# Attention and MoE in one kernel: a new issue order for a turn of the attention loop, and other engines for five of its copies out of PSUM

## The chip, the cores and the metric

The kernel runs on one core of one Trainium2 chip. The metric is the device time of one execution in microseconds (us): before the change the median of three runs is 442.36 us (441.19 to 442.59). The engines are named as in the profile: TensorE is PE (its weight loads PEld), VectorE is DVE, ScalarE is ACT, GpSimd is POOL, and SyncE, which issues most DMAs, is SP.

## The reference

Block-causal attention over 8 batches of 8 heads (576 positions, 64 per head, in float32), then a mixture of experts over the 4608 resulting tokens: a gate picks one of 8 experts per token, each expert keeps its 80 highest gates, and the kept tokens go through two matrix products.

```python
scores = scale * np.matmul(q, k.transpose(0, 1, 3, 2))           # q, k, v: (8, 8, 576, 64)
scores = np.where(block_i >= block_j, scores, -1000000000.0)      # blocks of 64 positions
attn = np.exp(scores - np.max(scores, axis=-1, keepdims=True))
attn = attn / (np.sum(attn, axis=-1, keepdims=True) + 1e-09)
x = np.matmul(attn, v)  # then (4608, 512): tokens by heads * 64
...
logits = x @ w_gate                                              # (4608, 8)
expert_idx, gate_w = argmax and its softmax probability
for e in range(8):
    tok_idx = the 80 tokens of expert e with the highest gate_w
    out[tok_idx] = gate_w[tok_idx, None] * (np.maximum(x[tok_idx] @ w1[e], 0) @ w2[e])
```

## The kernel before

The attention works on 32 pairs of heads (4 pairs per batch). A pair is spread over several turns of one loop: turn `i` loads pair `i+3`, turns the q and k of pair `i+1` (`prep`, DVE transposes at L409, q scaled on POOL at L412), makes the scores and the softmax of pair `i`, and finishes pair `i-1`. Four pairs of heads make a batch, and so four turns.

The rows of a pair's 576 positions are cut into tiles 0 to 3 of 128 rows and tile 4 of 64 rows. In a turn PE runs, in this order: the scores of tile 3 (`scores "3"`, L427), `back C` of the pair before (L492), the scores of tiles 2 and 0 (`"20"`), `back 44` (L475), `values 0` (L522), the scores of tile 1, `back A`, `values 1`, the scores of tile 4 (`scores_4`, L443), `back B`. A `back` turns exponentials by a product with the identity into PSUM; a `take` (L532 on ACT, L534 on DVE) copies it to SBUF, where `values` needs it: `back C` to the tile PF, `A` and `B` to PT, `44` to pl. `values` multiplies by v, and its own `take` copies the result to xT.

`max` (L448, and L452 for tile 4) finds the row maxima of the scores on DVE, `soft` (L456, L461) takes the exponentials on ACT, and reads the row sum with a second small instruction. `flip` (L275) transposes xT on DVE for storing.

The scores have two buffers in PSUM, used in rotation: the scores of tile 1 go where those of tile 3 were, so they wait for both `soft` of tile 3; those of tile 4 wait for the `soft` of tiles 2 and 0. `back C` needs tile 4's `soft` of the turn before, and `values 0` needs both halves of `back C` taken. All other products of PE in a turn rotate over four PSUM buffers (`pm`).

Every four turns a finished batch leaves nine small jobs in a list, and each `step` of the loop runs the next: `recip`, `store`, `logits` (two products, L292), `logits2` (five transposes, L304, and DVE work at L310 and L319), `gate` (nine DVE instructions, L327 to L341, with one exponential on ACT between, L330), `turn` (POOL) and `turn2` (L358, L362). So in turns 6, 10, ... come the first logits, in the next turn the rest of the logits, in the one after (8, 12, ..., 28; "the gate turn" below) the gate, and the fourth has no job. After turn 31 there is one more gate turn, 32, without new scores, and then the last batch is finished by itself.

Nothing is scheduled by a planner here: within the loop (`tc.manual_schedule()`, L564) every engine's queue holds its instructions in the order in which the table TURN calls them, and TAKE says which engine copies: `"a"` is ACT, `"v"` is DVE. What follows the loop (choice of the kept tokens, gather, experts) hangs on its end.

Of the kernel before, what the change touches and what calls it, by code (L numbers as in the profile page):

```python
# [24 lines left out]
CHUNK = 80  # L25


TAKE = {"back": {"A0": "a", "A1": "v", "B0": "a", "B1": "v", "C0": "a", "C1": "a", "44": "a"},
        "values": {0: "a", 1: "a"}}

GROUPS = {"3": ((3, 0),), "20": ((2, 0), (0, 384)), "1": ((1, 0),)}

TURN = (
    (3, "load"),
    (0, "begin"),
    (1, "prep", 0),
    (0, "scores", "3"),
    (-1, "back", "C"),
    (0, "scores", "20"),
    (-1, "take", "back", "C0"),  # L40
    (-1, "take", "back", "C1"),
    (2, "load_v"),
    (0, "max", "3"),
    (0, "soft", 3, 1),
    (0, "soft", 3, 0),
    (0, "max", "20"),
    (0, "step"),
    (-1, "back", "44"),
    (-1, "values", 0),
    (0, "soft", 0, 0),  # L50
    (0, "scores", "1"),
    (0, "soft", 2, 1),
    (0, "back", "A"),
    (1, "prep", 1),
    (-1, "take", "back", "44"),
    (0, "soft", 2, 0),
    (0, "max", "1"),
    (0, "take", "back", "A1"),
    (0, "soft", 0, 1),
    (-1, "take", "values", 0),  # L60
    (0, "soft", 1, 0),
    (0, "soft", 1, 1),
    (-1, "values", 1),
    (0, "scores_4"),
    (0, "back", "B"),
    (-1, "take", "values", 1),
    (-2, "flip"),
    (0, "max_4"),
    (0, "take", "back", "B1"),
    (0, "take", "back", "A0"),  # L70
    (0, "step"),
    (0, "soft_4"),
    (0, "take", "back", "B0"),
    (0, "step"),
)

# [2 lines left out]
def tile_attn_moe(ctx, tc, q, k, v, w_gate, w1, w2, capacity, out, xs=None, dbg=None):  # L79
# [295 lines left out]
    class Pair:  # L375
# [153 lines left out]
        def take(self, what, x):  # L529

            if TAKE[what][x] == "a":
                nc.scalar.copy(*self.out.pop((what, x)))  # L532
# [576 lines left out]
```

## Time and profile before

| | us |
|---|---|
| median of three runs | 442.36 |
| the profiled execution, device time | 441.93 |
| its span, first to last instruction | 440.2 |
| PE busy | 409.2 (93%) |
| ACT busy | 288.3 (65%) |
| DVE busy | 280.1 (64%) |
| POOL busy | 65.9 (15%) |

The loop fills the span from 8 to about 316 us. Shares of the whole span mix it with the experts, where DVE and ACT have little to do; inside the loop both are busy about 17 of every 20 us. The chain of waits that the page prints ends in the output's DMA and tells nothing of the loop, so the loop is read from the timeline, one engine at a time, where each row has its start, its length and, in brackets, the idle time before it with what ended it.

### The profile page before, as it was taken

To read this page: it belongs to the slowest core of one execution; us is meant where nothing else is said; L and a number is where in the kernel's file an instruction comes from. 1 tells how busy PE (TensorE), PEld (TensorE's weight loads), DVE (VectorE), ACT (ScalarE), POOL (GpSimd) and SP (SyncE) were. 2 spreads that over 40 slices of the span, in tenths; PEclk is the share of its full clock that TensorE was granted. 3 is DMA by queue.
4 is the path that set the end of the run, shared out by engine and by line. 5 is a ranking of instruction groups with operands and counts; after the bars stand their busy time and mean duration, and the time that the engine had idled before them with its cause. 6 is when DMAs were issued, how large, how long until landed. Compare 5 with 4: busy or idle time off the path is not lost. (4 is left out here: it accounts for less than half of the span.)

```text
span 440.2 us, 14257 instructions
## 1 busy us (share of the span) xinstructions
PE 409.2 (93%) x5755; PEld 263.4 (60%) x5755; DVE 280.1 (64%) x559; ACT 288.3 (65%) x887; POOL 65.9 (15%) x133
## 2 busy tenths in 40 slices
PE   5899999999999999999999999999868899999970
PEld 3466666666666566666666656666546855666510
DVE  5677788888798888879879887986682131100000
ACT  1698888798788879888887887888520123333230
POOL 5001111011111101112111010210026201100000
PEclk9899999999999999999999999999997899999996
DMA  9677878988786998898879887854087999999000
GB/s 130 117 133 165 174 125 212 241 171 165 190 164 130 158 291 171 167 210 178 170 136 281 167 173 192 179 128 110 2 224 245 324 405 410 412 401 357 20 15 21
DMA packets 230168, 84.34 MB, mean 192 GB/s; under 512 B 196877, under 2 KB 215309, under 8 KB 230096
## 3 DMA queue, kind: packets, MB, share of 16 engines
q1 hardware_dynamic: 222528, 64.91, 63.5%
q0 software_dynamic: 5200, 18.16, 11.9%
q8 instruction: 47, 0.77, 0.7%
q10 hardware_dynamic: 2368, 0.30, 0.6%
q14 instruction: 25, 0.20, 0.1%
HBM read 63.21 MB, written 20.33 MB: 190 GB/s over the span
## 5 line engine op out<-in xcount | busy, mean ns | idle before, releaser
L456 ACT ACTIVATE P<-sc,negm 128x128 f32<-128x128 f32 (+3 forms) x256 | 133.4, 531 | 16.2 <-DVE negm L448 14.5
L448 DVE TENSOR_REDUCE negm<-sc 128x2 f32<-128x1024 f32 (+3 forms) x128 | 100.6, 811 | 38.5 <-PE sc L434 38.4
L427 PE MATMUL sc<-T,T 64*128 64x128 f32 (+3 forms) x512 | 94.6, 468 | 2.2 <-POOL T L412 1.3
L492 PEld LDWEIGHTS pm<-ident,P 64*128 64x128 f32 x1536 | 56.4, 139 | 33.1 <-ACT xT L532 11.0
L492 PE MATMUL pm<-ident,P 64*128 64x64 f32 x1536 | 68.8, 229 | 1.9 <-DVE prod L310 0.4
L522 PE MATMUL pm<-PT,vn 128*64 128x128 f32 (+1 forms) x512 | 60.7, 379 | 0.0
L427 PEld LDWEIGHTS sc<-T,T 64*128 64x128 f32 x512 | 42.6, 191 | 23.7 <-issue 7.2
L412 POOL TENSOR_SCALAR T<-T 128x576 f32<-128x576 f32 x32 | 21.4, 668 | 227.0 <-DVE T L409 227.0
L456 ACT ACTIVATION_READ_ACCUMULATOR P<-sc,negm 128x1 f32 x256 | 52.6, 205 | 0.0
L409 DVE STREAM_TRANSPOSE T<-ld 128x576 f32<-128x576 f32 x64 | 48.7, 763 | 1.4 <-DMA ld<-in_q_dram 1.4
L522 PE MATMUL pm<-PF,vn 128*64 128x64 f32 (+1 forms) x768 | 48.2, 247 | 0.9 <-ACT PF L532 0.9
L522 PEld LDWEIGHTS pm<-PT,vn 128*64 128x64 f32 x512 | 33.5, 137 | 22.9 <-issue 22.9
L884 PE MATMUL av<-w,hT 128*32 128x512 f32 (+1 forms) x320 | 43.1, 594 | 1.6 <-DVE y L889 1.6
L532 ACT COPY PF<-pm 128x512 f32<-128x512 f32 x64 | 34.4, 588 | 15.0 <-PE pm L492 15.0
L843 PE MATMUL ps<-xsT,w 128*64 128x80 f32 x1024 | 40.7, 239 | 3.7 <-issue 3.7
L534 DVE COPY PT<-pm 128x512 f32<-128x512 f32 x64 | 43.5, 680 | 0.3 <-PE pm L492 0.3
L843 PEld LDWEIGHTS ps<-xsT,w 128*64 128x64 f32 x1024 | 38.3, 141 | 7.5 <-issue 7.0
L889 DVE SCALAR_TENSOR_TENSOR y<-av,comb,yt 80x512 f32<-80x512 f32 x8 | 6.0, 746 | 57.2 <-ACT yt L887 51.0
L443 PE MATMUL sc<-T,T 64*64 64x288 f32 x256 | 39.0, 424 | 1.2 <-ACT P L456 1.2
L461 ACT ACTIVATE P<-sc,negm 128x576 f32<-128x576 f32 x32 | 23.7, 741 | 22.1 <-DVE negm L452 22.1
L532 ACT COPY PT<-pm 128x512 f32<-128x512 f32 x64 | 37.8, 591 | 0.0
L522 PEld LDWEIGHTS pm<-PF,vn 128*64 128x64 f32 x768 | 32.0, 137 | 7.4 <-ACT PF L532 1.1
(168 smaller groups left out, 419.2 us busy)
## 6 DMA issues: line engine op xcount, KB each, us to landing
w<-in_moe_w_dram SPq DMA_DIRECT2D x13, 2048.0 KB, 19.2
ld<-in_q_dram SPq DMA_DIRECT2D x128, 72.0 KB, 3.2
out_dram<-zero POOLq DMA_DIRECT2D x18, 512.0 KB, 3.8
xs<-Y SPq DMA_DIRECT2D x32, 288.0 KB, 4.9
ld<-in_k_dram SPq DMA_DIRECT2D x124, 72.0 KB, 2.8
vn<-in_v_dram SPq DMA_DIRECT2D x64, 128.0 KB, 3.0
w<-in_moe_w_dram POOLq DMA_DIRECT2D x3, 2048.0 KB, 11.1
vt<-in_v_dram SPq DMA_DIRECT2D x32, 32.0 KB, 2.9
```

The lines of the kernel that those rows point to most:

```text
L409: nc.vector.transpose(t, self.nat[x].rearrange("p g d -> p (g d)"))
L427: nc.tensor.matmul(s[:, h, c:c + P * (u + 1)], lhsT=self.T[0][r, P * u:P * (u + 1)], rhs=self.T[1][r, 0:P * (u + 1)], start=(x == 0), stop ...
L443: nc.tensor.matmul(s[r, c, 0:288], lhsT=self.T[0][r, 512:S], rhs=self.T[1][r, 288 * c:288 * (c + 1)], start=True, stop=True)
L448: nc.vector.tensor_reduce(self.negm[:, u], self.s[g][:, :, c:c + P * (u + 1)], axis=AX.X, op=ALU.max, negate=True)
L456: nc.scalar.activation(Pt[self.i % 2][u][:, h], self.s[g][:, h, c:c + P * (u + 1)], AF.Exp, bias=self.negm[:, u, h:h + 1], scale=1.0, accu ...
L461: nc.scalar.activation(Pt[self.i % 2][4][:, 0:S].rearrange("p (c k) -> p c k", c=2), self.s["4"][:, :, 0:288], AF.Exp, bias=self.negm[:, 4 ...
L492: nc.tensor.transpose(pt[c][:, n_ * BLK:(n_ + 1) * BLK], from_[r, P * j:P * (j + 1)], ident[r, r])
L522: nc.tensor.matmul(to, lhsT=lhs, rhs=rhs, start=(n_ == 0), stop=(n_ == len(steps) - 1))
L532: nc.scalar.copy(*self.out.pop((what, x)))
L534: nc.vector.tensor_copy(*self.out.pop((what, x)))
L843: yield nc.tensor.matmul(dst(b)[64 * c:64 * (c + 1)], lhsT=w_[:, a, col:col + 64], rhs=x_[:, a], start=(a == 0), stop=(a == n - 1))
L884: last = nc.tensor.matmul(to[col:col + s1 - s0], lhsT=hT[:, a, s0:s1], rhs=w_[:, a], start=(a == ends[0]), stop=(a == ends[1]), tile_posit ...
```

## The change

The order of the calls in a turn is another, and five copies change their engine: `A1` and `B1` go from DVE to ACT; `B0`, `values 0` and `values 1` go from ACT to DVE.

```diff
-TAKE = {"back": {"A0": "a", "A1": "v", "B0": "a", "B1": "v", "C0": "a", "C1": "a", "44": "a"},
-        "values": {0: "a", 1: "a"}}
+TAKE = {"back": {"A0": "a", "A1": "a", "B0": "v", "B1": "a", "C0": "a", "C1": "a", "44": "a"},
+        "values": {0: "v", 1: "v"}}
...
     (0, "begin"),
-    (1, "prep", 0),
+    (0, "step"),
     (0, "scores", "3"),
...
+    (0, "soft_4"),
+    (0, "back", "B"),
+    (0, "take", "back", "B0"),
     (0, "take", "back", "B1"),
-    (0, "take", "back", "A0"),
-    (0, "step"),
-    (0, "soft_4"),
-    (0, "take", "back", "B0"),
     (0, "step"),
 )
```

A turn still has three `step`s. Before they stood in the middle (after the maxima of tiles 2 and 0), between `max_4` and `soft_4`, and at the end; now they stand at the start, in the middle (before `back 44`, with the maxima of tiles 2 and 0 behind it), and at the end. Both `prep`s now come after the maxima of tiles 2 and 0, and the `take` of `44` comes before the `soft` of tile 3. Beside the jobs' own products, the order of PE in a turn is unchanged.

On DVE, in a gate turn and the end of the turn ahead of it (`mx` to `Gm` is the gate; `negm x3` are the maxima of tiles 3, 2 and 0; `T` is a `prep`), before:

```order
L452 TENSOR_REDUCE negm<-sc 128x1
L534 COPY PT<-pm 128x2x2x128
L310 TENSOR_TENSOR prod<-pm,rs 128x256
L310 TENSOR_TENSOR prod<-pm,rs 64x64
L319 TENSOR_REDUCE lg<-prod 128x40
L409 STREAM_TRANSPOSE T_2087<-ld_1740 128x576
L448 TENSOR_REDUCE negm<-sc 128x2 x3
L327 TENSOR_REDUCE mx<-lg 128x5
L329 TENSOR_TENSOR dl<-lg,mx 128x5x8
```

And now, in the same place:

```order
L452 TENSOR_REDUCE negm<-sc 128x1
L534 COPY PT<-pm 128x2x2x128
L310 TENSOR_TENSOR prod<-pm,rs 64x64
L319 TENSOR_REDUCE lg<-prod 128x40
L327 TENSOR_REDUCE mx<-lg 128x5
L329 TENSOR_TENSOR dl<-lg,mx 128x5x8
...
L341 TENSOR_TENSOR Gm<-eq,g 128x40
L448 TENSOR_REDUCE negm<-sc 128x2 x3
L409 STREAM_TRANSPOSE T_2158<-ld_1740 128x576
L409 STREAM_TRANSPOSE T_2202<-ld_1741 128x576
L448 TENSOR_REDUCE negm<-sc 128x2
```

The whole gate moved from behind the maxima of tiles 3, 2 and 0 to ahead of them, one `prep` moved behind them, and the larger of the two L310 moved into the turn before.

On ACT, around the gate's exponential (`dl`; PF is `take` of `back C`, `P ... 128x512` the exponentials of tile 3), before:

```order
L461 ACTIVATE P_1_130,sums_1427<-sc,negm 128x576
L532 COPY PT<-pm 128x2x2x128
L532 COPY PF<-pm 128x512 x2
L456 ACTIVATE P_0_128,sums<-sc,negm 128x512 x2
L330 ACTIVATE dl<-dl 128x5x8
L456 ACTIVATE P_0_123,sums<-sc,negm 128x128
```

And now:

```order
L461 ACTIVATE P_1_130,sums_1427<-sc,negm 128x576
L532 COPY PT<-pm 128x2x2x128
L330 ACTIVATE dl<-dl 128x5x8
L532 COPY PF<-pm 128x512 x2
L532 COPY pl_132<-pm 64x128
L456 ACTIVATE P_0_128,sums<-sc,negm 128x512 x2
```

The gate's exponential moved ahead of the two copies of `back C`, and the copy of `44` ahead of the exponentials of tile 3.

## Rows read from the trace of the kernel before

**Rows 1.** The head of the page: the span, and PE's busy time, share of the span and instructions.

```profile
span 440.2 us, 14257 instructions
...
PE 409.2 (93%) x5755; PEld 263.4 (60%) x5755; DVE 280.1 (64%) x559; ACT 288.3 (65%) x887; POOL 65.9 (15%) x133
```

**Rows 2.** The timeline of PE, from a turn without jobs (it starts at 130.50) and the two starts that follow it, to a gate turn (159.14 to 168.38). Columns: start in us, us, engine, line, operation, out<-in, shape, count.

```profile
130.50 1.13 PE L427 MATMUL sc<-T,T 64*128 64x512 f32 x4
...
131.50 0.71 PE L492 MATMUL pm<-ident,P 64*128 64x64 f32 x16
...
139.27 1.08 PE L427 MATMUL sc<-T,T 64*128 64x512 f32 x4
...
140.52 0.71 PE L492 MATMUL pm<-ident,P 64*128 64x64 f32 x16
...
158.45 0.77 PE L304 MATMUL pm<-ident,lgT 128*128 128x128 f32 x5
159.14 1.13 PE L427 MATMUL sc<-T,T 64*128 64x512 f32 x4
...
160.13 0.70 PE L492 MATMUL pm<-ident,P 64*128 64x64 f32 x16
...
161.98 0.44 PE L522 MATMUL pm<-PF,vn 128*64 128x128 f32 x4
...
164.30 0.70 PE L427 MATMUL sc<-T,T 64*128 64x256 f32 x4
...
166.21 1.19 PE L443 MATMUL sc<-T,T 64*64 64x288 f32 x8
167.33 0.84 PE L492 MATMUL pm<-ident,P 64*128 64x64 f32 x16
...
168.38 0.70 PE L427 MATMUL sc<-T,T 64*128 64x512 f32 x2
```

**Rows 3.** The timeline of DVE over the same gate turn, from tile 4's maximum of the turn before (157.92) to tile 1's maximum (165.89); idle time before a row in brackets.

```profile
157.92 0.76 DVE L452 TENSOR_REDUCE negm<-sc 128x1 f32<-128x576 f32 x1 [0.41 <-PE sc L443]
158.60 0.68 DVE L534 COPY PT<-pm 128x512 f32<-128x512 f32 x1
159.19 0.54 DVE L310 TENSOR_TENSOR prod<-pm,rs 128x256 f32<-128x256 f32 x2
159.77 0.74 DVE L319 TENSOR_REDUCE lg<-prod 128x40 f32<-128x320 f32 x1
160.42 0.77 DVE L409 STREAM_TRANSPOSE T<-ld 128x576 f32<-128x576 f32 x1
161.11 2.38 DVE L448 TENSOR_REDUCE negm<-sc 128x2 f32<-128x1024 f32 x3
163.42 0.18 DVE L327 TENSOR_REDUCE mx<-lg 128x5 f32<-128x40 f32 x1
163.63 0.20 DVE L329 TENSOR_TENSOR dl<-lg,mx 128x40 f32<-128x40 f32 x1
...
165.19 0.78 DVE L409 STREAM_TRANSPOSE T<-ld 128x576 f32<-128x576 f32 x1
165.89 0.65 DVE L448 TENSOR_REDUCE negm<-sc 128x2 f32<-128x512 f32 x1
```

**Rows 4.** The timeline of ACT in the same gate turn: the copies of `back C`, the exponentials of tile 3 with the reading of their sums, the gate's exponential.

```profile
160.86 1.07 ACT L532 COPY PF<-pm 128x512 f32<-128x512 f32 x2 [0.83 <-PE pm L492]
162.42 0.69 ACT L456 ACTIVATE P<-sc,negm 128x512 f32<-128x512 f32 x1 [0.49 <-DVE negm L448]
...
163.10 0.68 ACT L456 ACTIVATE P<-sc,negm 128x512 f32<-128x512 f32 x1
163.67 0.20 ACT L456 ACTIVATION_READ_ACCUMULATOR P<-sc,negm 128x1 f32 x1
163.87 0.24 ACT L330 ACTIVATE dl<-dl 128x40 f32<-128x40 f32 x1
164.01 0.35 ACT L456 ACTIVATE P<-sc,negm 128x128 f32<-128x128 f32 x1
```

**Rows 5.** Groups of instructions over the whole span, shapes kept apart (busy us, mean ns of one): the maximum of tile 3, and the only copy on DVE out of PSUM that is about as small as that of `values 1`.

```profile
L448 DVE TENSOR_REDUCE negm<-sc 128x2 f32<-128x1024 f32 x32 | 38.3, 1195 | 3.9 <-PE sc L434 3.9
...
L362 DVE COPY Wt<-pm 128x40 f32<-128x40 f32 x8 | 1.7, 215 | 2.3 <-PE pm L358 2.3
```

**Rows 6.** The timeline of all engines at the last gate turn, 32, after the scores have ended: DVE's tile 4 maximum, a `flip`, the gate's first instruction, and the first of `values 0` with what it waited for.

```profile
309.45 0.76 DVE L452 TENSOR_REDUCE negm<-sc 128x1 f32<-128x576 f32 x1 [1.10 <-PE sc L443]
...
311.96 0.76 DVE L275 STREAM_TRANSPOSE Y<-xT 128x576 f32<-128x576 f32 x1
312.65 0.15 DVE L327 TENSOR_REDUCE mx<-lg 128x5 f32<-128x40 f32 x1
...
313.02 0.44 PE L522 MATMUL pm<-PF,vn 128*64 128x128 f32 x4 [0.88 <-ACT PF L532]
```

**Rows 7.** The timeline of the first turn on ACT and PE: the reading of tile 3's second sum, the scores of tile 1 behind it, the exponentials of tile 0 and the scores of tile 4.

```profile
12.97 0.20 ACT L456 ACTIVATION_READ_ACCUMULATOR P<-sc,negm 128x1 f32 x1
...
13.22 0.70 PE L427 MATMUL sc<-T,T 64*128 64x256 f32 x4 [0.97 <-ACT P L456]
...
13.68 0.37 ACT L456 ACTIVATE P<-sc,negm 128x128 f32<-128x128 f32 x1 [0.51 <-DVE negm L448]
...
15.67 0.75 PE L443 MATMUL sc<-T,T 64*64 64x288 f32 x2 [1.19 <-ACT P L456]
```

More of the change, by code (lines that the diff above doesn't have):

```diff
@@ L35 @@
     (0, "begin"),
-    (1, "prep", 0),
+    (0, "step"),
     (0, "scores", "3"),
     (-1, "back", "C"),
+    (-1, "take", "back", "C1"),
     (0, "scores", "20"),
+    (0, "max", "3"),
     (-1, "take", "back", "C0"),
[L41 to L46, printed above, removed]
     (0, "step"),
@@ L49 @@
     (-1, "values", 0),
+    (0, "max", "20"),
+    (-1, "take", "back", "44"),
+    (0, "soft", 3, 0),
+    (0, "soft", 3, 1),
+    (0, "soft", 2, 0),
+    (1, "prep", 0),
     (0, "soft", 0, 0),
+    (0, "soft", 0, 1),
+    (2, "load_v"),
     (0, "scores", "1"),
+    (0, "back", "A"),
+    (-1, "values", 1),
     (0, "soft", 2, 1),
-    (0, "back", "A"),
     (1, "prep", 1),
-    (-1, "take", "back", "44"),
-    (0, "soft", 2, 0),
     (0, "max", "1"),
-    (0, "take", "back", "A1"),
-    (0, "soft", 0, 1),
-    (-1, "take", "values", 0),
     (0, "soft", 1, 0),
     (0, "soft", 1, 1),
-    (-1, "values", 1),
+    (-1, "take", "values", 0),
     (0, "scores_4"),
-    (0, "back", "B"),
+    (0, "take", "back", "A0"),
+    (0, "take", "back", "A1"),
     (-1, "take", "values", 1),
```

## The prediction

> **What bounds the kernel now.** I read the head of the page first: PE is busy 93% of the span [rows 1], so what other engines do counts only where PE waits for it. The busy share doesn't show where that is, so I read PE's timeline by starts, turn against turn. A turn without jobs takes 139.27 - 130.50 = 8.77 us, the gate turn 168.38 - 159.14 = 9.24 [rows 2]. Inside them nearly every product starts as long after the one before as in all other turns; PE streams. Two waits are left. First, behind a turn without jobs `back C` starts 140.52 - 139.27 = 1.25 after the turn's start, where 131.50 - 130.50 = 1.00 is usual [rows 2]: it waits 0.25 for tile 4's exponentials. In PE's timeline I count 11 turns with it, seven behind a job-free one and four early ones. Second, in each of the six full gate turns (8, 12, ..., 28) the last `back B` loses about 0.13 (it lasts 0.84, where other `back`s last 0.71, [rows 2]). So no order can gain much more than 11 x 0.25 + 6 x 0.13 = 3.5 us in the loop; it can lose more, if it makes PE wait elsewhere.
>
> I therefore looked for the places with the least slack. One is `values 0`: `back C` ends at 160.13 + 0.70 = 160.83, the two copies to PF run 160.86 to 161.93, and `values 0` starts at 161.98 [rows 2, 4]. PE reaches it just when the copies are through, so any delay of these copies is PE's. The other is the scores of tile 1, which need the buffer of tile 3: the second sum of tile 3 is read by 163.67 + 0.20 = 163.87 [rows 4], PE follows 0.05 behind such a reading where it waits for it (13.17 to 13.22, [rows 7]), and reaches the place at 164.30 [rows 2]. Slack 0.38.
>
> **The change in an ordinary turn.** It removes two copies to PT from DVE (0.68 each) and one net copy of that size from ACT. DVE gets `B0`, of the same size, and two copies of `values`: the large one has 512 columns like those to PT, so 0.68 (0.58, ACT's time for such a copy, is the lower bound); the small one has 64 columns, and its nearest row is 0.215 for 40 columns on DVE [rows 5], with 0.68 as the upper bound. I take 0.22, by the nearer row. DVE thus has 0.2 more per turn. What these copies feed is late enough: between `values 1` and `back B`, which needs their buffers, lie the scores of tile 4 (1.12 us, 166.21 to 167.33, [rows 2]). Behind them on DVE stand `flip` and tile 4's maximum. Before, DVE idled 0.41 ahead of that maximum (157.92, [rows 3]), which covers the 0.2. The `take` of `44`, now ahead of tile 3's exponentials, has ACT wait some 0.1 us, and then copy 0.15, within the 0.38. The chain scores of tile 4, maximum, exponentials, `back C` keeps its links, so the 11 waits of 0.25 stay. Cost: nothing; without the cover, the excess of DVE in each of 31 turns.
>
> **The gate turn.** I lay both orders out from the start of tile 4's maximum in the turn before (157.92 is 0). Before, PE's turn starts at 159.14 - 157.92 = 1.22. Of the five transposes ahead of it (158.45 to 159.14, 0.69) four moved to the middle of that turn, so about 0.2 is left and the turn starts at 0.74. From there PE would reach `values 0` at 0.74 + (161.98 - 159.14) = 3.58 and the scores of tile 1 at 0.74 + (164.30 - 159.14) = 5.90 [rows 2].
>
> DVE, by starts in [rows 3]: maximum 0.68, copy to PT 0.59, the small L310 about 0.24 (of 0.58 for both), L319 0.65, in sum 2.16. Then comes the gate: its first instruction 0.21, the second 0.20, so ACT's exponential is free to go at 2.16 + 0.41 + 0.04 = 2.61 (163.87 against 163.83 before). The next ACT instruction follows 164.01 - 163.87 = 0.14 later [rows 4]. So the copies to PF, which now stand behind the exponential, start at 2.75. `back C` is through at 0.74 + 160.83 - 159.14 = 2.43, and they would have started at 2.46. `values 0` is late by 0.3.
>
> The whole gate lasts 165.19 - 163.42 = 1.77 [rows 3], so tile 3's maximum starts at 3.93 and ends 1.195 later [rows 5], at 5.12. Its exponentials start 162.42 - (161.11 + 1.195) = 0.12 later, the second follows by 0.68, its sum is read 163.87 - 163.10 = 0.77 after that [rows 3, 4], and PE goes on 0.05 behind: 5.12 + 0.12 + 0.68 + 0.77 + 0.05 = 6.74. The scores of tile 1 are late by 6.74 - 5.90 = 0.84; the 0.3 at `values 0` lies inside it.
>
> What follows: the second exponential of tile 3 leaves ACT at 5.12 + 0.12 + 2 x 0.68 = 6.60, two of tile 0 take 0.35 each [rows 4], two of tile 2 by an estimate between 0.35 and 0.68 0.57 each, in sum 8.45; PE comes to the scores of tile 4 at 6.74 + (166.21 - 164.30) = 8.65. Tile 1's maximum starts when DVE has done three maxima (2.31) and two `prep`s (0.7 each): 3.93 + 2.31 + 1.41 = 7.65; its two exponentials, by the same estimate 0.47 each, end by 9.5, `back B` starts at 6.74 + (167.33 - 164.30) = 9.77. So `back B` no longer waits: 0.13 back. DVE then has tile 1's maximum (0.65), the two copies of `values` (0.6 by starts, 0.22) and `flip` (0.69), and reaches tile 4's maximum at 9.8, when its scores end at 6.74 + 166.21 + 1.19 - 164.30 = 9.84: no slack, no loss. The net is 0.84 - 0.13 = 0.71 per gate turn, 6 x 0.71 = **4.3 us**. If DVE's gate overlapped the end of the turn before more than I assume, the loss is 0.3 (the copies alone) less 0.13; if DVE loses 0.3 at its end as well, it is 1.0. So 1.0 to 6.0 us.
>
> The rows of DVE and ACT stand in written order throughout [rows 3, 4]. The Trainium skill, "PSUM — Partial Sum Buffer", section "Engine vs sequencer instructions", says that the queues of both engines are strictly first in, first out. By that rule this loss can't be passed by a ready copy; were it false, the 4.3 us would be 0.
>
> **The other jobs** have the same products on PE as before: the logits now stand side by side, the transposes apart. I take 0, between -0.1 and 0.1 per batch. DVE's large L310 now runs behind tile 3's maximum in a turn whose PE work is half a microsecond longer in the middle, so nothing waits for it. `recip` before tile 3's maximum is four small instructions, by the gate's 0.21 each [rows 3] about 0.9, within a turn whose `back C` is 0.25 late as well: 0.
>
> **The end and the start.** Gate turn 32 has no scores, and PE already waits there 0.88 us for the copies to PF before `values 0` at 313.02, that is 313.02 - 309.45 = 3.57 after tile 4's maximum [rows 6]. Now these copies wait for the gate: 2.16 as above, a `flip` of 312.65 - 311.96 = 0.69, 0.41 and 0.04 to the exponential, 0.14 to the copies, 1.07 for them, 0.05 to PE: 4.55. That is **1.0 us** later, and everything behind the loop hangs on it. Whether the four transposes, which lay in that wait before, cost 0.5 more I leave to the range. In the first turn ACT waited 0.51 for tile 0's maximum and PE 1.19 for it at tile 4's scores (15.67, [rows 7]); with tile 2 first, ACT does not wait for tile 0's maximum, which is some 0.4 long: **-0.4 us**, between -0.5 and 0.
>
> **Sum.** 4.3 + 1.0 - 0.4 = 4.9 on the profiled execution's own 441.93 (span 440.2): 446.8 us. That execution lies 0.4 below the median of 442.36.
>
> **Rivals.**
> - *The gate is hidden.* If DVE begins the gate about 0.8 us earlier than I laid it out, tile 3 meets its 0.38 and only the end and the start count: 441.93 + 1.0 - 0.4 = 442.5. For it: in the loop DVE is not full. Against: from 158.60 on no row of DVE in the gate turn has idle time before it [rows 3].
> - *Faster.* `back C` gets tile 4's exponentials sooner and `back B` its own: 441.93 - 3.5 = 438.4. For it: both waits exist. Against: tile 4's maximum already finds DVE idle for 0.41 and starts with its scores' end, so nothing in the order can bring it forward. Busy isn't speed: the Trainium skill, "Trainium Kernel Development and Optimization", section "Best Practices", says that matmul busy share should not be used as distance from the roofline. By that rule more could be won than the waits; the equal starts of all turns say no here.
> - *DVE bounds every turn.* If the small copy costs its upper bound of 0.68, or waits for `values 1` long enough, `flip` ends 0.25 after tile 4's scores, and each of 31 turns is late by that: 7.8 more, 446.8 + 7.8 = 454.6. It decides once DVE's additions exceed 0.41. Against: 0.2 by the nearer rows.
>
> **Chances.** The forecast 0.72, hidden 0.14, faster 0.08, DVE in every turn 0.06. A measurement of this kernel tells 0.3% (1.3 us) from no change. The forecast's own range is 443.5 to 449.5. The hidden case lies about the bound between same and slower: faster 0.08, same 0.13, slower 0.79. The range of 442.2 to 449.6 leaves out the faster case and DVE in every turn.
>
> **What would show it.** In the new profile the gate turns should take 9.9 to 10.0 us from start to start, with `values 0` about 3.15 and the scores of tile 1 about 6.0 after the turn's start, and a wait of the tile 1 scores for ACT that hardly existed. Turns without jobs should stay at 8.77, and `back C` at 1.25 behind them. `values 0` of turn 32 should wait about 1.9 instead of 0.88. Gate turns of 9.3 or less would refute the layout of DVE; longer turns everywhere would speak for the last rival.

## The result, and the profile after

The changed kernel takes 447.56 us (median of four runs, 446.94 to 448.41), the kernel before, run beside it, 442.12 (441.19 to 442.59). The ratio is 1.0134 with a 95% interval of 1.0114 to 1.0155. So the change makes the kernel slower, by 1.3%; forecast were 446.8 us and 442.2 to 449.6. Of the experiments below, one (one job in each turn) has four of 13 executions at 443.2 to 445.6 us, where the other nine took 436.4 to 439.5; its median is of all 13, its ratio of the nine.

The head of the page of the kernel after, to hold against [rows 1]: the span is 6.5 us longer (446.7 against 440.2), and PE is busy as long as before.

```profile
span 446.7 us, 14298 instructions
...
PE 409.6 (92%) x5755; PEld 263.4 (59%) x5755; DVE 288.9 (65%) x591; ACT 285.5 (64%) x855; POOL 65.6 (15%) x133
```

PE is idle for 446.7 - 409.6 = 37.1 us, where it was for 31.0, so the loss is nearly all waiting. The page's part on the costliest groups of the kernel after shows two waits on PE (behind the bar: busy time and mean ns, then the idle time ahead of the group and what ended most of it):

```profile
L427 PE MATMUL sc<-T,T 64*128 64x128 f32 (+3 forms) x512 | 94.7, 469 | 4.8 <-ACT P L456 3.6
...
L522 PE MATMUL pm<-PF,vn 128*64 128x64 f32 (+1 forms) x768 | 48.7, 249 | 4.3 <-ACT PF L532 4.3
```

Scores now wait 3.6 us for exponentials, and `values` 4.3 us for the copies to PF (0.9 before). Where that is, PE's timeline shows, here the gate turn 12, from its start at 121.94 to the next turn's, and `back C` in the turn that follows the job-free one:

```profile
121.94 1.13 PE L427 MATMUL sc<-T,T 64*128 64x512 f32 x4
...
125.20 0.44 PE L522 MATMUL pm<-PF,vn 128*64 128x128 f32 x4 [0.37 <-ACT PF L532]
...
128.04 0.70 PE L427 MATMUL sc<-T,T 64*128 64x256 f32 x4 [0.46 <-ACT P L456]
...
131.08 0.71 PE L492 MATMUL pm<-ident,P 64*128 64x64 f32 x16
...
132.00 1.13 PE L427 MATMUL sc<-T,T 64*128 64x512 f32 x4
...
140.75 1.08 PE L427 MATMUL sc<-T,T 64*128 64x512 f32 x4
...
141.99 0.28 PE L492 MATMUL pm<-ident,P 64*128 64x64 f32 x2
```

The gate turn takes 132.00 - 121.94 = 10.06 (9.24 in [rows 2]). `values 0` starts 125.20 - 121.94 = 3.26 after the turn's start and the scores of tile 1 at 6.10; in [rows 2] the same two stand at 2.84 and 5.16. Two waits, one behind the other, neither of which was there. `back B` lasts 0.71, so its old half wait (0.84) is gone. The job-free turn takes 140.75 - 132.00 = 8.75, and `back C` behind it still comes at 141.99 - 140.75 = 1.24.

Why PE waits is read from DVE and ACT. DVE of the kernel after in the same gate turn, from tile 4's maximum (against [rows 3]):

```profile
121.18 0.76 DVE L452 TENSOR_REDUCE negm<-sc 128x1 f32<-128x576 f32 x1
121.86 0.68 DVE L534 COPY PT<-pm 128x512 f32<-128x512 f32 x1
...
122.69 0.76 DVE L319 TENSOR_REDUCE lg<-prod 128x40 f32<-128x320 f32 x1
123.48 0.20 DVE L327 TENSOR_REDUCE mx<-lg 128x5 f32<-128x40 f32 x1
123.71 0.20 DVE L329 TENSOR_TENSOR dl<-lg,mx 128x40 f32<-128x40 f32 x1
...
125.09 0.20 DVE L341 TENSOR_TENSOR Gm<-eq,g 128x40 f32<-128x40 f32 x1
125.21 2.41 DVE L448 TENSOR_REDUCE negm<-sc 128x2 f32<-128x1024 f32 x3
127.54 1.43 DVE L409 STREAM_TRANSPOSE T<-ld 128x576 f32<-128x576 f32 x2
128.89 0.65 DVE L448 TENSOR_REDUCE negm<-sc 128x2 f32<-128x512 f32 x1
```

And ACT of the kernel after (against [rows 4]):

```profile
123.95 0.24 ACT L330 ACTIVATE dl<-dl 128x40 f32<-128x40 f32 x1 [0.67 <-DVE dl L329]
124.09 1.05 ACT L532 COPY PF<-pm 128x512 f32<-128x512 f32 x2
...
126.54 0.69 ACT L456 ACTIVATE P<-sc,negm 128x512 f32<-128x512 f32 x1 [1.25 <-DVE negm L448]
```

ACT stands idle for 0.67 with `back C` ready, because the gate's exponential is ahead of its copies and waits for DVE's second gate instruction. Then it stands idle for 1.25, because DVE finishes the gate before it finds tile 3's maximum (125.21). No row of DVE here has idle time before it.

Over the loop the starts of the turns add up as follows. The six full gate turns are 0.82 longer, one of them 0.92 (+5.0). The seven turns that now hold both logits products (6, 10, ..., 30) take 10.23 instead of 9.89 (+2.3), and the six behind them (7, 11, ..., 27) 9.51 instead of 9.98 (-2.8). Turn 31 starts 4.56 later (305.26 against 300.70). The rest of the 6.5 us comes in turn 32 and behind it.

### The profile page after: what moved, and what is told of

Read it like the earlier page. It is cut to its first block, busy times and chain, and to the rows that moved or that the text cites. A ratio compares the mean times of both kernels' runs of the same rounds, so it can differ in the third digit from the quotient of the medians.

```text
span 446.7 us, 14298 instructions
## 1 busy us (share of the span) xinstructions
PE 409.6 (92%) x5755; PEld 263.4 (59%) x5755; DVE 288.9 (65%) x591; ACT 285.5 (64%) x855; POOL 65.6 (15%) x133
## 5 line engine op out<-in xcount | busy, mean ns | idle before, releaser
L456 ACT ACTIVATE P<-sc,negm 128x384 f32<-128x384 f32 (+3 forms) x256 | 131.0, 524 | 24.3 <-DVE negm L448 24.0
L492 PE MATMUL pm<-ident,P 64*128 64x64 f32 x1536 | 67.8, 228 | 2.3 <-ACT P L461 0.8
L522 PE MATMUL pm<-PT,vn 128*64 128x128 f32 (+1 forms) x512 | 61.9, 385 | 0.0
L532 ACT COPY PT<-pm 128x512 f32<-128x512 f32 x96 | 52.9, 592 | 0.0
L409 DVE STREAM_TRANSPOSE T<-ld 128x576 f32<-128x576 f32 x64 | 45.6, 751 | 0.5 <-DMA ld<-in_q_dram 0.5
L534 DVE COPY xT<-pm 128x512 f32<-128x512 f32 x64 | 28.9, 451 | 5.5 <-PE pm L522 4.0
```

The lines of the kernel that those rows point to most:

```text
L409: nc.vector.transpose(t, self.nat[x].rearrange("p g d -> p (g d)"))
L456: nc.scalar.activation(Pt[self.i % 2][u][:, h], self.s[g][:, h, c:c + P * (u + 1)], AF.Exp, bias=self.negm[:, u, h:h + 1], scale=1.0, accu ...
L492: nc.tensor.transpose(pt[c][:, n_ * BLK:(n_ + 1) * BLK], from_[r, P * j:P * (j + 1)], ident[r, r])
L522: nc.tensor.matmul(to, lhsT=lhs, rhs=rhs, start=(n_ == 0), stop=(n_ == len(steps) - 1))
L534: nc.vector.tensor_copy(*self.out.pop((what, x)))
```

## The experiments

Every ratio is to the kernel before on the same chip. The kernel before has medians from 438.57 to 442.12 us in these comparisons, so ratios and turns are compared, not the times themselves. "A, B, C, D" are the four turns of a batch: the first logits, the next turn, the gate turn, the job-free turn. Before they take 9.90, 9.98, 9.24 and 8.77, in sum 37.9; after 10.23, 9.51, 10.06 and 8.75, in sum 38.55.

**The place of one step alone.** In the kernel before:

```diff
     (0, "begin"),
+    (0, "step"),
     (1, "prep", 0),
...
     (0, "take", "back", "A0"),
-    (0, "step"),
     (0, "soft_4"),
```

> The kernel before with one line moved: the step between the maximum and the exponentials of tile 4 now stands at the start of the turn; copies, maxima, exponentials and preps as before. Theory (the gate ahead of tile 3's maximum is the loss): DVE now has the gate and a prep ahead of that maximum, so the gate turns get 0.7 us longer than in the changed kernel, about 10.7 us, and turn 32 waits for the copies of back C about 1.9 us; median 450 to 454 us. Rival (the new engines of the five copies, or the new order of the exponentials, are the loss): gate turns stay at 9.2 to 9.4, median 441.5 to 443.5.

Measured: 454.79 us, ratio 1.0295 (1.0254 to 1.0335), just above the expected 450 to 454. A 10.22, B 9.51, C 10.88 (10.7 was expected). PE in its gate turn 12, which starts at 122.45:

```profile
125.71 0.44 PE L522 MATMUL pm<-PF,vn 128*64 128x128 f32 x4 [0.37 <-ACT PF L532]
...
129.32 0.70 PE L427 MATMUL sc<-T,T 64*128 64x256 f32 x4 [1.22 <-ACT P L456]
```

The step's place by itself makes both waits, and makes the second longer than in the kernel after, since here a `prep` too stands ahead of tile 3's maximum. It costs more than the whole change: the rest of the change gives some of it back.

**The gate late.** In the kernel after, the gate runs behind the maxima of tiles 2 and 0, as before; all other jobs stay (the start step waits if the gate is next):

```diff
     (0, "soft", 3, 1),
+    (0, "gate"),
...
```

> The changed kernel with the gate alone moved: it is not taken by the steps at the start or in the middle, but runs behind the exponentials of tile 3 and the maxima of tiles 2 and 0; everything else of the change stays. Theory: tile 3's exponentials and the copies of back C are no longer late, gate turns 9.1 to 9.4 us, values 0 of turn 32 waits under 1 us, median 441 to 443.5. Rival (copies and order of the exponentials): median 445.5 or more, gate turns near 10.

Measured: 446.78 us, ratio 1.013 (1.011 to 1.015), by time no different from the kernel after. A miss. `values 0` (2.85) and the scores of tile 1 (5.16) are back in their places, but C still takes 9.74. DVE shows where it went:

```profile
121.21 0.76 DVE L453 TENSOR_REDUCE negm<-sc 128x1 f32<-128x576 f32 x1
...
123.39 2.56 DVE L449 TENSOR_REDUCE negm<-sc 128x2 f32<-128x1024 f32 x3
...
127.68 1.44 DVE L410 STREAM_TRANSPOSE T<-ld 128x576 f32<-128x576 f32 x2
129.04 0.65 DVE L449 TENSOR_REDUCE negm<-sc 128x2 f32<-128x512 f32 x1
...
129.62 0.80 DVE L535 COPY xT<-pm 128x512 f32<-128x512 f32 x2
...
131.03 0.72 DVE L453 TENSOR_REDUCE negm<-sc 128x1 f32<-128x576 f32 x1
```

and ACT and PE of the same kernel, where the wait has gone:

```profile
129.79 0.47 ACT L457 ACTIVATE P<-sc,negm 128x256 f32<-128x256 f32 x1 [1.36 <-DVE negm L449]
...
130.70 1.07 ACT L533 COPY PT<-pm 128x512 f32<-128x512 f32 x2
```

```profile
130.44 0.89 PE L493 MATMUL pm<-ident,P 64*128 64x64 f32 x16 [0.20 <-DVE xT L535]
131.43 0.35 PE L359 MATMUL pm<-sp,sameR 128*32 128x40 f32 x16
```

From tile 4's maximum to the next one DVE works 131.03 - 121.21 = 9.82 us, without a gap that the rows show. Both `prep`s now stand between the gate and tile 1's maximum, and with none ahead of tile 3's maximum DVE comes too early for the scores of tiles 2 and 0: its three maxima take 2.56 instead of 2.38 [rows 3]. Tile 1's maximum comes 129.04 - 121.97 = 7.07 after the turn's start (165.89 - 159.14 = 6.75 in [rows 3]), and tile 1's exponentials are late by as much.

`back B` starts at 130.44, 8.47 after the turn's start instead of 8.19. It needs the first of these exponentials (through at 129.79 + 0.47 = 130.26) and the buffer of `values 0`, whose `take` is new on DVE and stands behind the late maximum (129.62 + 0.68 = 130.30). The profile names the copy, which came last. But `back B` starts 0.65 after the exponential does, and so it does in the last experiment below, where its first product isn't held by that copy. So the exponential is enough to explain it.

The turn's end hangs on neither. `turn2` waits for the first of the two copies of `back A`, now both on ACT, which stand behind tile 1's exponentials: the copy starts at 130.70, `turn2` 0.73 later. The wait had only moved, along the chain from tile 1's maximum over its exponentials and that copy to `turn2`.

**The gate cut in two.** In the kernel after, `mx`, `dl` and the exponential stay in the start step, and the other seven DVE instructions run behind the maxima of tiles 2 and 0.

```diff
     (0, "max", "20"),
+    (0, "gate2"),
...
```

> The changed kernel with the gate cut in two: its first two DVE instructions and its exponential on ACT stay at the start of the turn, the other seven DVE instructions go behind the maxima of tiles 2 and 0. Theory of two parts: the exponential ahead of the copies of back C alone makes values 0 late by 0.3 to 0.4 us (it starts 3.2 to 3.3 after the turn's start), the scores of tile 1 then follow without a wait of their own (5.5 to 5.6 after the turn's start instead of 6.1), and turn 32 keeps its long wait; median 444 to 446.5. If the exponential's place costs nothing: 441.5 to 443.5. If it is the whole loss: 447 to 448.

Measured: 446.76 us, ratio 1.0149 (1.0089 to 1.0209); C 9.72, `values 0` at 3.26, the scores of tile 1 at 5.58. The places are as expected: the first wait belongs to the exponential ahead of the copies, the second to the other seven instructions. The time, just above what was expected, can't decide it: its executions reach from 444.7 to 450.3, and its interval holds that of the kernel after. `turn2` starts at 9.44, behind `back B` at 8.61 and the same wait for ACT, of which the next experiment but one tells more.

**Only the last gate late.** In the kernel after, the gate is late in turn 32 alone (`i >= n`).

> The changed kernel with only the last batch's gate (turn 32) moved behind the copies of back C; the six gate turns in the loop stay as changed. Theory: turns 0 to 31 keep their times (gate turns 10.06), values 0 of turn 32 waits about 0.9 instead of 1.93, and its products are not run at half the granted clock; median 1.5 to 3 us below the changed kernel, 444.5 to 446. Rival (the end is not on the path, or the half clock comes anyway): 446.5 to 448.

Measured: 445.70 us, ratio 1.0102 (1.0066 to 1.0137), as expected, though the interval overlaps that of the kernel after. C stays at 10.06; `values 0` of turn 32 starts 12.31 after turn 31 does, where the kernel after has 13.30 and the kernel before 12.32. So the last gate's place costs 1.0 there. The products behind it run at full clock, which the last section shows not to follow from the gate's place alone.

**The copies alone.** In the kernel before, the new TAKE, with the `take` of A1 put beside that of A0, and B0 and B1 in exchanged places.

> The kernel before with the five copies on their new engines and nothing else of the new order, but that B0 and B1 change places and A1 stands beside A0, so that no engine waits for a copy it could take later. Theory (the places of the jobs are the loss, the copies cost nothing): gate turns 9.2 to 9.4 us, other turns as before, median within 0.3% of before, 440 to 443. Rival (DVE has no room for the two copies of values): gate turns 9.6 or more, or every turn 0.2 longer, median 3 us or more above before.

Measured: 440.49 us, ratio 1.0052 (1.0022 to 1.0081), where within 0.3% was expected. A, B and D as before; C 9.42 (9.2 to 9.4 was expected). Ordinary turns pay nothing, as forecast, but each gate turn pays 0.18, in six turns 1.1 us or 0.25%; the rest of the 0.5% isn't located. Only `turn2` is late in the gate turn, 9.13 after the turn's start instead of 8.96. PE of this kernel, in a gate turn that starts at 121.52:

```profile
129.70 0.84 PE L492 MATMUL pm<-ident,P 64*128 64x64 f32 x16
130.65 0.35 PE L358 MATMUL pm<-sp,sameR 128*32 128x40 f32 x16
```

And ACT of the same kernel ahead of it:

```profile
129.92 1.07 ACT L532 COPY PT<-pm 128x512 f32<-128x512 f32 x2
```

Both copies of `back A` are now on ACT behind tile 1's exponentials, and `turn2` starts 0.73 after they do. The list of PE's instructions with their waits gives `turn2` a wait for the first of these copies; in the kernel before its wait is for the small copy of `values 1`. `turn2` starts 1.64 after the first of tile 1's exponentials, in this run, in those with the late and the cut gate and in three below, all with the new copies; with the old ones in the old order 1.46 to 1.47 (the kernel before, and the run with a filler behind each turn). That is the 0.18.

**The jobs as before, all else new.** The kernel with the late gate, and its start step moved to the end of the turn.

```diff
     (0, "begin"),
-    (0, "step"),
...
     (0, "step"),
+    (0, "step"),
 )
```

> The changed kernel with the jobs where they were: the first step goes to the end of the turn, beside the last one, and the gate runs behind the exponentials of tile 3. Copies, preps, maxima and exponentials stay as changed. Theory (the run with only the gate late stayed slow because the second logits product still lengthens the turn of the logits by 0.33 us, while the 0.47 saved in the next is lost again behind DVE): turns of a batch come back to 9.9, 10.0, 9.2 to 9.4 and 8.75 us; ratio to before 0.997 to 1.004. Rival (the new order of preps and exponentials, or the copies, cost as well): gate turn 9.6 or more, ratio 1.006 or more.

Measured: 440.66 us, ratio 1.0069 (1.0042 to 1.0095). A 9.90, B 9.98, C 9.75. The rival held: with every job where it was, the new order of `prep`s, maxima and copies costs 0.5 per gate turn (0.34 by tile 1's late maximum, 0.18 by the copies); tile 1's maximum is at 7.09, `back B` at 8.48 and `turn2` at 9.47, as in the run with the late gate. DVE shows why the maximum is late here:

```profile
123.08 1.29 DVE L449 TENSOR_REDUCE negm<-sc 128x2 f32<-128x768 f32 x2 [0.21 <-PE sc L435]
```

It waits for the scores of tiles 2 and 0, where before a `prep` filled that time. In the kernel after all this is hidden under the larger loss: tile 1's maximum is at 128.89 - 121.94 = 6.95 there, and `turn2` comes 2.04 after the first of tile 1's exponentials, where 1.64 is enough (1.64 in the runs with the copies alone and with the late gate).

**One job in each turn.** The kernel before, jobs spread so that every turn ends in one with a PE product: `recip`, `store`, first logits | nothing, nothing, second logits | nothing, both `logits2` | gate, `turn`, `turn2` (with a third buffer for the sums).

> The kernel before with its jobs spread, so that between the last product of a turn and the first of the next there is always a job's product: first logits, second logits, transposes, and the gate's last product one turn later than before; the last batch keeps its old places. If the wait of back C behind a turn without a job can be filled: back C starts 1.0 instead of 1.25 us after each of those turns' starts, a batch of four turns takes 37.4 to 37.5 instead of 37.88 us, ratio to before 0.992 to 0.996. If DVE, which has no idle time around the gate, gives it back: ratio 0.998 to 1.002.

Measured: 437.93 us, ratio 0.9995 (0.9975 to 1.0014). A 9.64, B 9.29, C 9.53, D 9.24, in sum 37.7. `back C` is at 1.00 in every turn, as expected, but only 0.2 of 0.4 per batch is won, and the ratio is the one that was expected if DVE gives it back. The profiled execution is one of the four long ones: one turn (25) took 14.07, because its q came late (`prep` waited 3.76 for the DMA) and the granted clock fell behind that pause. So turns and not spans are compared here; whether the other three had the same isn't known.

**A filler behind each turn.** The same, but with the second logits in the middle of B, the larger half of the transposes at its end, and the smaller at the end of C.

> The kernel before with its order and copies kept; only the list of jobs is spread so that each of the four turns of a batch ends in a job with a PE product: recip, store, first logits | second logits in the middle, nothing, larger half of the transposes at the end | nothing, nothing, smaller half | gate, turn, turn2. (As in the experiment with one job each turn, but with the second logits product back in the middle of its turn.) My theory: the only waits of PE in the loop before are back C behind a job-free turn (0.25) and 0.13 in the gate turn, so the four turns of a batch go from 37.88 to about 37.5 or 37.6 (9.64, 9.75, 8.95, 9.25), seven times, and the ratio is 0.992 to 0.997. Rival: a job at a turn's end always costs PE more than in the middle, because its own wait replaces the one that it fills; then a batch takes 37.7 to 37.9 as in the experiment before, and the ratio is 0.998 to 1.002.

Measured: 443.29 us, ratio 1.003 (1.0008 to 1.0052). A 9.64, B 9.87, C 9.06, D 9.38, in sum 37.95: a miss. `back C` waits nowhere, and yet nothing is won. In D, where the gate is now, `back B` lasts 0.92 and `turn2` follows it, and the transposes cut in two take 0.66 + 0.30 where they took 0.77 together [rows 2]. So the 0.25 that PE waits behind a job-free turn couldn't be had by filling it in either of these two ways.

**The kernel after with the jobs spread.** `turn2` of the last batch, `recip` and `store`, first logits | nothing, second logits, larger half | nothing, nothing, smaller half | nothing, nothing, gate behind the maxima, `turn`.

> The kernel after with its order and copies kept, but with the jobs spread: turn2 of the last batch, then recip and store, then first logits | nothing, second logits in the middle, larger half of the transposes at the end | nothing, nothing, smaller half | nothing, gate behind the maxima of tiles 2 and 0, turn at the end; turn 32 has its gate there too. My theory: the new order loses because the gate stands ahead of the copies to PF and of tile 3's maximum, and where it doesn't, because DVE is full in the turn that has the gate and the smaller half of the transposes' work; with the gate alone in its turn, that turn (the fourth) takes 9.0 to 9.4, a batch 37.5 to 37.9, and the ratio is 0.994 to 1.002. Rival: the new order of prep, maxima and copies itself fills DVE in any turn with a gate, whatever else is in it; then the fourth turn takes 9.6 or more, a batch 38.0 or more, and the ratio is 1.004 or more.

Measured: 446.03 us, ratio 1.0103 (1.0074 to 1.0133). A 9.63, B 9.86, C 9.07, D 9.74. My theory fell, the rival held: also with a gate turn that has hardly another job, tile 1's maximum comes at 7.06, `back B` at 8.46 and `turn2` at 9.46, as in the run with the late gate.

**The first prep back.** The kernel with the late gate, and one `prep` again at the turn's start.

```diff
     (0, "begin"),
+    (1, "prep", 0),
     (0, "step"),
...
-    (1, "prep", 0),
```

> The kernel after with the gate behind the maxima of tiles 2 and 0 (as in the experiment on the late gate), and the first prep back at the start of the turn, as before the change. Steps, exponentials and copies are those of the kernel after. Theory: what kept the gate turn at 9.74 with a late gate is that both preps stand between the gate and tile 1's maximum, so that DVE comes 0.7 late to that maximum and back B waits for its exponentials; with one prep ahead, the gate turn takes 9.3 to 9.5, the turns of a batch 10.23, 9.51, 9.42 and 8.75, in sum 37.9, and the ratio is 0.999 to 1.005. Rival: it is the two copies of values, new on DVE in that turn; then the gate turn stays at 9.6 or more, and the ratio is 1.008 or more.

Measured: 445.79 us, ratio 1.0098 (1.0072 to 1.0125), which is the rival's; C 9.56, between the two expectations. Tile 1's maximum is at 6.89, `back B` at 8.29 and `turn2` at 9.28. So the second `prep` ahead of that maximum was 0.18 of the 0.5 (9.74 - 9.56). The rest is 9.56 - 9.24 = 0.32: 0.18 for the copy that `turn2` now waits for, as in the run with the copies alone, and 0.14 because tile 1's maximum is at 6.89 and not 6.75. DVE's way from tile 4's maximum to this one has even become shorter (7.65 against 165.89 - 157.92 = 7.97, [rows 3]), but PE, with the transposes moved, starts the gate turn 0.76 instead of 1.22 after tile 4's maximum. A rose to 10.37, for here `recip` and a `prep` both stand ahead of tile 3's maximum.

**The old copies in the new order.** The same, with the TAKE of before.

> As the kernel with the prep back, but with the copies on the engines that they had before the change. The theory that the copies cost 0.18 per gate turn: the gate turn takes 9.24 to 9.3, the batch about 37.75 against 37.88 before, and the ratio is 0.996 to 1.001, up to 0.004 below the kernel with the prep back and the new copies. Rival: without the other copies the new order of exponentials makes ACT late in the gate turn; then the gate turn takes 9.5 or more, and the ratio is not below that of the other kernel.

Measured: 451.71 us, ratio 1.0234 (1.0208 to 1.0261). C 10.08 and A 10.57: a clear miss. PE in a gate turn that starts at 83.58:

```profile
90.66 1.19 PE L444 MATMUL sc<-T,T 64*64 64x288 f32 x8
91.85 0.24 PE L493 MATMUL pm<-ident,P 64*128 64x64 f32 x1
92.75 0.71 PE L493 MATMUL pm<-ident,P 64*128 64x64 f32 x15 [0.66 <-ACT xT L533]
```

and ACT of the same kernel at that place:

```profile
91.20 0.47 ACT L457 ACTIVATE P<-sc,negm 128x256 f32<-128x256 f32 x1 [0.72 <-DVE negm L449]
...
91.67 0.47 ACT L457 ACTIVATE P<-sc,negm 128x256 f32<-128x256 f32 x1
...
92.11 0.58 ACT L533 COPY xT<-pm 128x512 f32<-128x512 f32 x1
```

In the new order the `take` of `values 0` stands behind tile 1's exponentials. On ACT it then starts when the last of them leaves (92.11). The first product of `back B` starts 91.85 - 91.20 = 0.65 after the first exponential; the other fifteen wait for the buffer until the copy is through (92.11 + 0.58). On DVE that copy is through in time, as the same 0.65 in the run with the late gate shows. So the two halves of the change belong together: the new copies cost 0.5% in the old order, and save 1.4% in this new one with the gate late (1.0234 against 1.0098).

No run beats the kernel before by more than its interval.

## Why the prediction was right, point by point

- **PE streams, and only waits count.** Right in the main: PE's busy time is nearly unchanged (409.6 against 409.2), and the loss stands in two rows of waits. But the sum of busy times hides what cancels: the half waits of `back B` (6 x 0.13) counted as busy and are gone, and turn 32's products at half clock (see the end) are new.
- **An ordinary turn costs nothing.** Right for the turns 2 to 5 (9.02 against 9.01) and for the job-free turn. The small copy to xT takes 224 ns by its group (0.22 was taken, with 0.68 as the bound), and the large one 679; the idle time ahead of tile 4's maximum falls from 0.41 to 0.14 in the turns without jobs, so the cover held. But the step didn't look at the gate turn: there the copies cost 0.18 by themselves. They feed `back B`, which the step named, and, through the rotation of the buffers, `turn2`, which it didn't.
- **The gate turn.** Right in both mechanisms and nearly in size. Forecast: `values 0` at 3.15, the scores of tile 1 at 6.0, net 0.71; measured: 3.26, 6.10 and 0.82. The first gate instruction starts 0.79 after the row ahead of it (123.48 - 122.69), not 0.65, and that is the 0.1. The run with the gate cut in two shows that the two waits are two: without the other seven instructions the second starts at 5.58 instead of 6.1. That ACT's ready copies stood still for 0.67 behind a waiting exponential agrees with the Trainium skill, "PSUM — Partial Sum Buffer", section "Engine vs sequencer instructions": the queues of these engines are first in, first out.
- **The other jobs.** Wrong step, small effect: "I take 0, between -0.1 and 0.1 per batch". The logits side by side make A 0.34 longer, and B gets 0.47 back: a batch gains 0.13, and the loop 2.8 - 2.3 = 0.5. The bound was a little too narrow, and neither turn by itself is unchanged.
- **The end.** The wait of `values 0` in turn 32 was forecast as 1.9 and is 1.93. PE of the kernel after there:

```profile
316.33 0.30 PE L475 MATMUL pm<-ident,P 128*64 128x128 f32 x1
318.56 0.44 PE L522 MATMUL pm<-PF,vn 128*64 128x128 f32 x4 [1.93 <-ACT PF L532]
318.83 3.12 PE L522 MATMUL pm<-PT,vn 128*64 128x384 f32 x16
```

  What the step lacked is the third row: the sixteen products take 3.12, not 1.90 as in the kernel before. More on this below; it adds up to 1.7 us, of which the profiled execution shows 0.7 given back further on (the lag is 7.2 at the end of `values` and 6.5 at the end of the span).
- **The first turn.** Wrong: "-0.4 us". Turn 0 takes 10.48 against 10.40. ACT of the kernel after, the last exponential of tile 3 and the first of tile 2:

```profile
12.39 0.68 ACT L456 ACTIVATE P<-sc,negm 128x512 f32<-128x512 f32 x1
...
13.76 0.58 ACT L456 ACTIVATE P<-sc,negm 128x384 f32<-128x384 f32 x1 [0.60 <-DVE negm L448]
```

  It starts 0.10 after tile 0's maximum ends (DVE's pair runs from 12.37 to 13.66), though tile 2's was through long before. The list of ACT's instructions with their waits tells why: the first exponential of tile 2 waits for DVE, and the two of tile 0 behind it carry no wait of their own, so that one wait covers both maxima. The scores of both tiles lie side by side in the same 512 columns of PSUM (GROUPS puts tile 0 at column 384). The Trainium skill, "PSUM — Partial Sum Buffer", section "PSUM bank collisions raise a hardware error", says that two engines must not touch the same bank in the same partitions at the same time, not even both to read, and that the compiler back end adds a dependency between them. The trace agrees, with the 0.10; no run here put the two tiles apart, so the reason isn't shown. That the maxima also share the tile negm isn't it: above, tile 3's exponentials start at 126.54, while the maxima of tiles 2 and 0, in the same tile, run on to 127.62.

```
L456 ACTIVATE P_0_126,sums<-sc,negm 128x384 [waits DVE_49,PE_49]
L456 ACTIVATE P_0_123,sums<-sc,negm 128x128 x2
L456 ACTIVATE P_0_126,sums<-sc,negm 128x384
```

- **The sum.** Forecast: 4.3 + 1.0 - 0.4 = 4.9. Profiled: 5.0 in the gate turns, -0.5 in the other jobs, +0.1 in the first turn, 1.0 in turn 32's wait, 1.0 net from the slow products behind it: 6.6, of 6.5. The medians differ by 5.4. So the total is better than its parts, and some of its closeness is luck: the errors in the first turn (0.5) and in the jobs (0.5) cancel, the gate turns were 0.7 too small, and the clock was no term at all.
- **The rivals.** *Hidden* failed as the timeline said: DVE has no idle time there. *DVE bounds every turn* failed (turns 2 to 5 are unchanged), but a full DVE is real in the gate turn, where four kernels with a late gate and the new copies still take 9.56 to 9.75. *Faster* failed, and two kernels that fill the wait of 0.25 gain nothing that the runs can tell either.

## What to carry to other kernels

Where an in-order queue feeds an engine that streams, an instruction that waits belongs behind everything that is ready, and a block of small instructions of which one result is needed belongs behind the one that another engine needs soonest. When a wait is removed, look at once for the next one on the same engine: here the late gate cured both waits and left 0.5 of the gate turn's 0.82, because tile 1's maximum came late from a full DVE, and a product at the turn's end now needed a copy on ACT behind that tile's exponentials. And where the profile names the engine that came last, ask whether the product would have started earlier without it. An order and an assignment of engines should be tested together and apart, since each alone can point the wrong way.

## What the runs showed of the hardware

The granted clock of TensorE fell to half (1.2 of 2.4 GHz) in turn 32 of the kernel after. Its windows (us, busy time and instructions of PE, PEld, DVE, ACT, POOL, then the granted clock, DMA share, GB/s):

```profile
312.00:319.30 7.30, 4.52 (x74) 3.06 (x72) 5.55 (x17) 4.76 (x15) 0.81 (x2) 1.00 0.01 2
319.30:322.75 3.45, 3.45 (x32) 2.36 (x28) 0.34 (x1) 0.00 (x0) 0.24 (x1) 0.51 0.00 0
322.75:327.00 4.25, 3.90 (x58) 2.78 (x55) 3.79 (x13) 0.70 (x2) 0.00 (x0) 1.00 0.07 4
```

It fell some 0.8 us after PE had taken up work again behind the wait of 1.93. The longer wait isn't the whole reason: of all thirteen kernels the clock fell there in the three with a wait of 1.93 to 1.94 (after, the step alone, the gate cut in two), but also in one of the ten with a wait of 0.88 to 0.94. That one is the kernel with the gate late everywhere:

```profile
312.00:316.20 4.20, 2.41 (x44) 1.68 (x42) 3.70 (x10) 3.38 (x9) 0.25 (x1) 1.00 0.01 4
316.20:319.60 3.40, 3.40 (x22) 1.82 (x18) 0.70 (x4) 0.00 (x0) 0.79 (x1) 0.51 0.00 0
```

The kernel with only the last gate late has the same busy time of PE before it (2.41 in 4.20) and keeps the full clock:

```profile
312.00:316.20 4.20, 2.41 (x42) 1.46 (x38) 3.48 (x9) 3.46 (x10) 0.25 (x1) 1.00 0.02 4
316.20:319.20 3.00, 3.00 (x57) 2.21 (x61) 1.52 (x7) 0.20 (x2) 0.79 (x1) 1.00 0.00 0
```

What decides between the two stays open. At the start it is alike: in nine kernels the first four scores of tile 3 run at half clock (2.07 to 2.08) and turn 0 takes 10.2 to 10.5; in four they run at full clock (1.13) and it takes 8.6 to 9.0. In two of these four it is down when turn 1 starts, and turn 1 takes 10.1 and 10.2, where it takes 8.7 to 9.2 in the others. Such a stretch is worth up to 2 us in a single execution, more than the loss of one gate turn (0.82), and is a reason to compare turns rather than spans.
